# Top-k attention with a highway layer on one core: the joint rest group moved forward, the end of the program re-ordered, a sum moved into SBUF

## The chip, the cores and the metric

The kernel runs on one core of one Trainium2 chip. Its time is the device time of one execution in microseconds (us). Before the change the median of three runs is 880.23 us (879.85 to 880.78). The profiled execution took 880.15 us; its span from the first to the last instruction is 878.4 us, so some 1.8 us lie outside the span.

The engines are named as in the profile: PE is TensorE (PEld its weight loads), DVE is VectorE, ACT is ScalarE, POOL is GpSimd and SP is SyncE, which here only starts transfers.

## What is computed

Inputs are `q`, `k` and `v` of 8 batches, 8 heads, 576 positions and 64 dimensions, and the weights of one layer of width 512. Cut to what matters:

```python
scores = matmul(q, k.T) / sqrt(64)                # (8, 8, 576, 576)
kth    = 32nd largest score of each row
attn   = softmax(where(scores >= kth, scores, -1e9))
x      = matmul(attn, v), heads side by side      # (4608, 512)
H = maximum(x @ w_h, 0)
T = sigmoid(x @ w_t + b_t)
out = T * H + (1 - T) * x                         # (4608, 512) float32
```

The kernel works with `x + (tanh((x @ w_t + b_t) / 2) + 1) * d`, where `d = max(x/2 @ w_h, 0) - x/2`, which is the same value.

## The kernel before

**Tiles and groups.** A batch has 576 queries: four full query tiles of 128 rows and a rest of 64 rows. A `Group` is one query tile of one batch with all its heads. A full group has eight score tiles of 128 queries by 576 keys, one for each head. In a rest group two heads share a tile, 64 rows each, so it has four tiles. The work goes in *pairs* of two tiles: four pairs in a full group, two in a rest group, 144 in all. Two pairs make a *quad*, 72 in all. Two neighbouring batches share the output rows of their rest groups: the second batch's rest group fills rows 64 to 127 of the same buffer, and the *joint* group of 128 rows then goes through the layer once. There are therefore 36 passes through the layer: 32 of full groups and 4 joint ones. The list `groups` (line 762) sets the order, batch by batch, the four full groups and then the rest.

**A pair's way.** PE makes the scores into a PSUM tile of four banks (`scores`, pool `bigps`, one buffer), and ACT moves their positive part into an SBUF buffer `z` (`evac`). Selecting the 32nd largest value of each row is DVE's work. `tree` takes the larger of the two halves of a row (`hi`, one instruction for each pair). `folds` does this twice more for a whole quad (`hh`, `h3`, and the smaller ones into `w2`), and POOL derives the smaller partners in `minima` by exact integer subtraction and addition, four instructions for a quad. `tops` and `rest` are chains of `max` (eight largest values of each row) and `match_replace` over these folded lists. Their last result, `m4`, holds the threshold. `mask` lets ACT write a penalty `pen` for values below it. PE transposes `z` and `pen` together into `zt` and `zr` (`parts`), ACT takes the exponential into `et`, and PE multiplies it with the values (`av`), 20 matmuls of 64 output rows for a pair of a rest group and 10 of 128 for a pair of a full one. ACT copies the result into `xs`.

**The layer of a group.** `norm` takes the reciprocal of the row sums on DVE and multiplies on POOL, which gives `x`. In the loop it then starts the write of `x` to the output in HBM on SP. `ffn_x` transposes `x` on PE, and ACT makes `xT` and `xh`, minus half of `x`. `ffn_h` and `ffn_r` multiply with `w_h` and take the positive part into `d` on ACT, and `ffn_d` adds `xh` to `d` by an accumulating transfer that POOL starts. For joint groups and the last two groups (`late`) one DVE instruction does both. `ffn_t` multiplies with `w_t`, and ACT takes the tanh in PSUM. `ffn_e` (DVE) multiplies, and `ffn_o` adds `d` to the rows already in HBM by accumulating transfers of POOL: one for a full group, two for a joint one, as its rows belong to two batches. The last two groups (`last`) add on an engine instead and write once. For the group before the last, `gp`, DVE also makes the product `x` and `xT`, and POOL makes `xh`.

**What sets the order.** Every engine takes its instructions in program order. The order is written by hand: the loop at line 873 advances one pair in each of 145 steps. In step `n` it folds pair `n`, scores pair `n+1`, selects older pairs, transposes pair `n-4` and multiplies pair `n-5`. `x`, `h` and `t` of the layer are put into a list `ffn` and taken one in each step, `x` in odd steps. If the `t` of one group is followed by the `x` of another, `ffn_x` of the latter is run in the same step, ahead of the transposes of pair `n-4` (lines 895 and 945); this is how a joint group, whose sums are ready two steps after those of the full group ahead of it, comes in. The program behind the loop (lines 960 to 1008) finishes the last three pairs by hand. There `gl` is the last group (before: the joint group of batches 6 and 7, two pairs) and `gp` the one before it (before: the fourth full group of batch 7). Four banks of one `bigps` tile serve as spare PSUM: three for `gp`'s layer, one for the end of the last transposes, and two of them again for `gl`'s `final_t`.

**What decides at the very end** whether the exact second version of the program is needed is computed from `room` and `scales` (`judge_lists`, `judge_scales`, `judge`). It is not needed with these inputs.

Of the kernel before, what the change touches and what calls it, by code (L numbers as in the profile page):

```python
# [9 lines left out]
ALU = mybir.AluOpType  # L10
AX = mybir.AxisListType
FP32 = mybir.dt.float32
# [7 lines left out]
J = 4  # L20
# [47 lines left out]
class Ops:  # L68


    def __init__(self, ctx, tc, shared, exact):
        self.tc = tc
        self.nc = tc.nc if exact else PinnedCore(tc)
        self.__dict__.update(shared)
        self.exact = exact
        s = "g" if exact else ""

        def pool(name, bufs, **kw):
            return ctx.enter_context(tc.tile_pool(name=name + s, bufs=bufs, **kw))

        PS = bass.MemoryType.PSUM
        self.ldpool = pool("ld", 2 if exact else 3)
        self.kqpool = pool("kq", 1 if exact else 2)
        self.scpool = pool("sc", 2) if exact else None
        self.treepool = pool("tree", 3)
        self.wpool = pool("w", 4)
        self.lpool = pool("l", 2)
        self.etpool = pool("et", 2)
        self.xpool = pool("x", 2)
        self.fpool = pool("f", 2)  # L90
        self.bigps = pool("bigps", 1, space=PS)
        self.ztps = pool("ztps", 2, space=PS)
        self.zrps = pool("zrps", 1, space=PS)
        self.fps = pool("fps", 1, space=PS)
        self.st = {}
        self.quads = {}
        self.spare = []

# [147 lines left out]
    def minima(self, k, after):  # L248


        H1, H2 = self.S // 2, self.S // 4
        gp, S = self.nc.gpsimd, self.S
        hi, hh, h3 = self.quads[k]
        z = self.zbufs[k % NZ]
        sci, hii, hhi = [a[:].bitcast(I32) for a in (z, hi, hh)]
        if k == 0:
            head = gp.tensor_tensor(hii, sci[:, :, 0:H1], hii, ALU.subtract)
        else:
            head = gp.tensor_tensor(hhi, hii[:, :, 0:H2], hhi, ALU.subtract)
        self.tc.add_manual_dep(  # L260
            head.ins,
            after.ins.name,
            mybir.DependencyInfo(
                mybir.DependencyClass.Sync, mybir.DependencyReason.DATA
            ),
            reason="after the folds",
        )
        if k:
            gp.tensor_tensor(hhi, hhi, hii[:, :, H2:H1], ALU.add)
            gp.tensor_tensor(hii, sci[:, :, 0:H1], hii, ALU.subtract)  # L270
        gp.tensor_tensor(hii, hii, sci[:, :, H1:S], ALU.add)
# [211 lines left out]
    def norm(self, g):  # L483
        nc, P, H, D = self.nc, self.P, self.H, self.D
        ql = g.rows
        xs3 = g.xs[0:ql, :].rearrange("p (h e) -> p h e", e=D + 1)
        rinv = self.scales[:, g.gi, :]
        nc.vector.reciprocal(rinv[0:ql, :], xs3[:, :, D])
        g.x = self.xpool.tile([P, H * D], FP32, tag="x", name="x")
        x3 = g.x[0:ql, :].rearrange("p (h d) -> p h d", h=H)  # L490
        for hs in (slice(0, H // 2), slice(H // 2, H)) if g.final else (slice(0, H),):
            (nc.vector if g.last else nc.gpsimd).tensor_tensor(
                x3[:, hs, :],
                xs3[:, hs, 0:D],
                rinv[0:ql, hs].unsqueeze(2).to_broadcast([ql, hs.stop - hs.start, D]),
                ALU.mult,
            )
        if g.added:
            for i, dst in enumerate(g.outs):
                n = ql // len(g.outs)  # L500
                nc.sync.dma_start(dst, g.x[i * n : (i + 1) * n, :])

    def final_x(self, g):

# [39 lines left out]
    def final_o(self, g, dsts, queues):  # L544


        vec, P = self.nc.vector, self.P
        W = self.dm // 2
        n = P // len(dsts)
        o = self.fpool.tile([P, self.dm], FP32, tag="o", name="o")  # L550
        for j, tp in enumerate(g.tp):
            cs = slice(j * W, (j + 1) * W)
            vec.scalar_tensor_tensor(
                out=g.d[:, cs], in0=tp, scalar=1.0, in1=g.d[:, cs],
                op0=ALU.add, op1=ALU.mult,
            )
            vec.tensor_tensor(o[:, cs], g.x[:, cs], g.d[:, cs], ALU.add)
            for i, dst in enumerate(dsts):
                queues[i].dma_start(dst[:, cs], o[i * n : (i + 1) * n, cs])

    def ffn_bank(self, g, name, other=False):
        if g.last and not g.final:
            return self.spare.pop(0)
        if g.final or other:
            return self.ztps.tile([self.P, 512], FP32, tag="zt", name=name)
        return self.fps.tile([self.P, 512], FP32, tag="fp", name=name)

    def ffn_x(self, g):
        nc, P, n_g, ql = self.nc, self.P, self.n_g, g.rows
        xtps = self.ffn_bank(g, "xtps", g.joint)  # L570
        for i in range(n_g):
            nc.tensor.transpose(
                xtps[:, i * P : i * P + ql],
                g.x[0:ql, i * P : (i + 1) * P],
                self.ident[0:ql, 0:ql],
            )
        g.xT = self.fpool.tile([P, n_g, P], BF16, tag="xT", name="xT")
        xt3 = xtps[:].rearrange("p (g j) -> p g j", j=P)[:, :, 0:ql]
        if g.last:
            nc.vector.tensor_scalar_mul(g.xT[:, :, 0:ql], xt3, 0.5)  # L580
        else:
            nc.scalar.mul(g.xT[:, :, 0:ql], xt3, 0.5)
        g.xh = self.fpool.tile([P, self.dm], FP32, tag="xh", name="xh")
        if g.last:
            nc.gpsimd.tensor_scalar_mul(g.xh[0:ql, :], g.x[0:ql, :], -0.5)
        else:
            nc.scalar.mul(g.xh[0:ql, :], g.x[0:ql, :], -0.5)

    def ffn_h(self, g):
        nc, P, n_g, ql = self.nc, self.P, self.n_g, g.rows  # L590
# [63 lines left out]
    def ffn_o(self, g, *dsts):  # L654
        ql = g.rows
        n = ql // len(dsts)
        if g.added:
            for i, dst in enumerate(dsts):
                self.nc.gpsimd.dma_start(
                    dst, g.d[i * n : (i + 1) * n, :], accum_op=ALU.add  # L660
                )
            return
        o = self.fpool.tile([self.P, self.dm], FP32, tag="o", name="o")
        self.nc.gpsimd.tensor_tensor(o[0:ql, :], g.x[0:ql, :], g.d[0:ql, :], ALU.add)
        for i, dst in enumerate(dsts):
            self.nc.sync.dma_start(dst, o[i * n : (i + 1) * n, :])
# [3 lines left out]
def kernel(  # L670
# [10 lines left out]
    nc = tc.nc  # L681
    P = nc.NUM_PARTITIONS
    B, H, S, D = q.shape
# [8 lines left out]
    nck = J + 1  # L692
# [21 lines left out]
    for i in range(2):  # L714
# [15 lines left out]
        P=P, H=H, S=S, D=D, R=R, NHP=NHP, n_g=n_g, dm=dm,  # L730
# [5 lines left out]
    with ExitStack() as cm:  # L736
# [18 lines left out]
        def out_rows(g):  # L755
            if not g.rem:
                r0 = g.b * S + g.qt
                return [out[r0 : r0 + JP : J, :]]
            ends = [(g.b + i) * S for i in (0, 1)]
            return [out[r1 - R : r1, :] for r1 in ends]  # L760
# [1 line left out]
        groups = [  # L762
            Group(b, qt, b * nck + qt, H, P, joint=True)
            for b in range(B)
            for qt in range(nck)
        ]
        groups[-1].final = True
        for i, g in enumerate(groups):
# [95 lines left out]
        def attend(m):  # L864
            ops.mask(m, *pairs[m])
            values(m - 1)
            ops.trans(m)

        def values(m):
            g, pi = pairs[m]  # L870
            ops.av(m, g, pi, preps[g.b]["vb"])

        while step <= NPR:
# [83 lines left out]
                ffn += [("x", g), ("h", g), ("t", g)]  # L957
            step += 1

        (kind, fg), = ffn  # L960
        assert kind == "t" and not pieces
        m, (gp, gl) = NPR - 3, groups[-2:]
        ops.ffn_t(fg)
        attend(m)
        late = ops.lists_rest(m // 2 + 1, *pairs[m + 1])
        gens, late = late[0:2], late[2:]
        ops.run(gens)
        ops.mask(m + 1, *pairs[m + 1])
        ops.ffn_e(fg)
        ops.ffn_o(fg, *out_rows(fg))  # L970
        ops.run(late)
        big = ops.bigps.tile([P, 2, 1024], FP32, tag="big", name="ps")
        banks = [
            big[:, i // 2, i % 2 * 512 : (i % 2 + 1) * 512] for i in range(4)
        ]
        ops.spare = banks[0:3]
        values(m)
        part, ends = ops.parts(m + 1)
        part(0)
        ops.mask(m + 2, *pairs[m + 2], tis=(0,))  # L980
        part(1)
        ops.mask(m + 2, *pairs[m + 2], tis=(1,))
        ends()
        ops.norm(gp)
        ops.settle(gl)
        part, ends = ops.parts(m + 2, banks[3])
        ends()
        part(0)
        values(m + 1)
        ops.ffn_x(gp)  # L990
        part(1)
        judge_lists()
        values(m + 2)
        ops.norm(gl)
        ops.ffn_h(gp)
        ops.ffn_r(gp)
        ops.final_x(gl)
        ops.ffn_d(gp)
        ops.ffn_t(gp)
        judge_scales()  # L1000
        ops.ffn_e(gp)
        ops.ffn_o(gp, *out_rows(gp))
        ops.ffn_h(gl)
        ops.ffn_r(gl)
        ops.ffn_d(gl)
# [78 lines left out]
```

## Time and profile before

| view of the profile | what it shows |
|---|---|
| busy share of the span | DVE 96%, PE 80%, ACT 79%, POOL 79% |
| windows of 110 us between 112 and 772 us | DVE busy 109.31 to 109.38 us in each |
| window 834 to 846 us | DVE busy 11.73 of 12.00 us |
| window 846 to 860 us | DVE busy 10.18 of 14.00 us |
| window 860 us to the end | DVE busy 8.39, PE 7.56, ACT 3.56 us |
| last selecting instruction of DVE (`m`) | ends at 856.39 us |
| last compute instruction (`o` on DVE) | ends at 872.19 us |
| granted PE clock | 0.954 over the span, 0.80 from 860 us on |

All compute instructions pass through one helper, so they carry line 35, and the profile's groups are told apart by the names of their tiles: `hh<-hi` is a fold, `x<-xs,scales` the product of `norm`, `d<-hps,xh` the `ffn_d` of a joint group. A group's row reads: engine, operation, output and input with shapes, how often; then busy time in us, mean ns of one; then the time the engine was idle ahead of them and who ended that. A timeline's row reads: start in us, duration in us, engine and instruction, and in brackets the idle time ahead of it and its releaser. Durations of instructions that follow each other on an engine overlap a little, as they are pipelined; from start to start a `d` costs DVE 0.59 us though its duration is 0.69.

### The profile page before, as it was taken

The page shows a single profiled execution, that of the slowest core. Times are in us where ns is not written, and L with a number is a line of the kernel's source. Part 1 is how long each engine was busy: PE and PEld are TensorE (multiplying, and loading weights), DVE is VectorE, ACT ScalarE, POOL GpSimd, SP SyncE. Part 2 cuts the span into 40 slices and gives each one's busy share as a digit, 9 for nine tenths or more (in the row PEclk, how much of TensorE's full clock was granted, in tenths as well). Part 3 has the DMA queues.
Part 4 walks back from the last instruction along what each step waited for, and adds up shares of the span by engine and source line. Part 5 has one row for each costly group of instructions (what it writes and reads, how often), then busy time and mean ns, then how long its engine had stood idle before and what let it go on. Part 6 is the DMA issues. An engine that isn't in the chain of part 4 may idle for free.

```text
span 878.4 us, 19848 instructions
## 1 busy us (share of the span) xinstructions
PE 704.7 (80%) x6524; PEld 497.8 (57%) x6569; DVE 847.3 (96%) x4201; ACT 694.9 (79%) x1243; POOL 695.8 (79%) x451
## 2 busy tenths in 40 slices
PE   6777988878787888778788787887988778877884
PEld 4555565655555556555566555665655555655652
DVE  4999999999999999999999999999999999999994
ACT  4787978888788897788788887887878888777873
POOL 5788887888878888788887888888887888878861
PEclk9799999999999999999999999999999999898888
DMA  9553413233143332234234341223313211111121
GB/s 201 123 109 69 102 37 61 67 65 89 29 85 69 72 84 49 62 59 102 41 70 76 67 108 24 52 66 73 97 38 61 38 34 29 38 25 25 38 40 37
DMA packets 104702, 57.32 MB, mean 65 GB/s; under 512 B 82192, under 2 KB 91792, under 8 KB 104592
## 3 DMA queue, kind: packets, MB, share of 16 engines
q1 hardware_dynamic: 92768, 37.37, 16.7%
q0 software_dynamic: 10608, 18.22, 13.7%
q8 instruction: 53, 0.87, 0.4%
q10 hardware_dynamic: 1216, 0.39, 0.2%
q14 instruction: 57, 0.47, 0.2%
HBM read 30.67 MB, written 18.35 MB: 56 GB/s over the span
## 4 chain that ended last, share of the span: by engine, by line
DVE 93%; PE 2%; ACT 2%; issue 1%; SPq 1%; DMA 0%; DVEq 0%; ACTq 0%
DVE w L35 50%; DVE m L35 19%; DVE hi L35 11%; DVE hh L35 7%; DVE h L35 4%; DVE d L35 3%; PE ps L35 1%; PE zt L35 1%; ACT pen L35 1%; SPq L35 1%; ACT et L35 0%; DMA qin<-in_q_dram 0%; DVE scales L35 0%; ACT z L35 0%; PE zr L35 0%
## 5 line engine op out<-in xcount | busy, mean ns | idle before, releaser
L35 PE MATMUL ps<-kq 64*128 64x64 f32 (+3 forms) x1280 | 215.9, 463 | 93.5 <-DVE hi L35 89.2
L35 ACT ACTIVATE z<-ps 128x1152 f32<-128x1152 f32 x144 | 163.2, 1134 | 111.3 <-PE ps L35 108.9
L35 ACT ACTIVATE pen<-z,m 128x576 bf16<-128x576 f32 x288 | 226.2, 786 | 0.1
L35 PE MATMUL zt<-ident,z 128*128 128x128 f32 x1152 | 223.4, 287 | 0.3
L35 PEld LDWEIGHTS ps<-kq 64*128 64x128 f32 (+1 forms) x1280 | 108.7, 186 | 194.4 <-DVE hi L35 100.4
L35 PE MATMUL zt<-nident,pen 128*128 128x128 bf16 x1152 | 212.8, 224 | 0.0
L35 POOL TENSOR_TENSOR hh<-hi,hh 128x576 int32<-128x576 int32 x71 | 100.4, 1414 | 133.4 <-DVE w L35 133.4
L35 POOL TENSOR_TENSOR hi<-z,hi 128x1152 int32<-128x1152 int32 x72 | 189.4, 2631 | 14.0 <-DVE m L35 8.5
L35 POOL TENSOR_TENSOR hi<-hi,z 128x1152 int32<-128x1152 int32 x72 | 191.1, 2654 | 5.6
L35 PEld LDWEIGHTS zt<-ident,z 128*128 128x128 f32 x1152 | 168.4, 146 | 18.3 <-ACT xT L35 1.0
L35 ACT ACTIVATE et<-zt 128x512 bf16<-128x512 f32 x288 | 161.4, 606 | 12.3 <-PE zt L35 11.5
L35 DVE MAX8 m<-w 128x8 f32<-128x168 f32 x576 | 161.1, 323 | 0.0
L35 PEld LDWEIGHTS <-pen 128*128 128x128 bf16 x1440 | 159.1, 111 | 2.9 <-ACT pen L35 2.8
L35 DVE MAX8 w<-hi 128x8 f32<-128x288 f32 x288 | 116.8, 448 | 0.1
L35 DVE TENSOR_TENSOR hi<-ps,z 128x576 f32<-128x576 f32 x144 | 108.0, 750 | 5.8 <-ACT z L35 5.8
L35 POOL TENSOR_TENSOR hh<-hh,hi 128x576 int32<-128x576 int32 x71 | 100.2, 1411 | 5.6
L35 PE MATMUL zr<-v,et 128*128 128x65 bf16 (+1 forms) x1580 | 89.4, 196 | 18.6 <-ACT et L35 14.7
L35 PEld LDWEIGHTS <-et 128*128 128x128 bf16 (+1 forms) x1600 | 70.0, 102 | 59.5 <-ACT et L35 45.4
L35 DVE MATCH_REPLACE8 w<-m,w 128x168 f32<-128x168 f32 x288 | 89.7, 321 | 0.0
L35 DVE MAX8 w<-hh 128x8 f32<-128x72 f32 x576 | 85.2, 234 | 0.0
L35 PE MATMUL zr<-ident,z 128*128 128x128 f32 x286 | 73.9, 312 | 2.3 <-ACT xs L35 2.3
L35 DVE TENSOR_TENSOR hh<-hi 128x576 f32<-128x576 f32 x73 | 58.6, 803 | 2.5
(91 smaller groups left out, 1120.9 us busy)
## 6 DMA issues: line engine op xcount, KB each, us to landing
vin<-in_v_dram SPq DMA_DIRECT2D x8, 1024.0 KB, 5.6
kin<-in_k_dram SPq DMA_DIRECT2D x63, 128.0 KB, 3.1
qin<-in_q_dram SPq DMA_DIRECT2D x63, 128.0 KB, 3.1
out_dram<-x SPq DMA_DIRECT2D x31, 256.0 KB, 2.9
d<-xh POOLq DMA_DIRECT2D x31, 256.0 KB, 3.6
out_dram<-d POOLq DMA_DIRECT2D x31, 256.0 KB, 4.2
krest<-in_k_dram SPq DMA_DIRECT2D x8, 128.0 KB, 3.9
qrest<-in_q_dram SPq DMA_DIRECT2D x8, 128.0 KB, 4.9
```

Of the source, the lines that this page charges most:

```text
L35: return self._tc.keep_in_program_order(fn(*args, **kw))
```

## The change

1. In the last batch the rest group is taken second, after the first full group. The joint group of batches 6 and 7 then passes through the layer in the loop, like the other three, and the last two groups `gp` and `gl` are both full.
2. Behind the loop `bigps` is closed and four one-bank PSUM tiles take its place. `gp`'s layer starts right behind the loop and is spread over the last three pairs; `gl`'s layer follows alone. ACT makes `xT` and `xh` of `gp`, and POOL its `x`.
3. The product `x` of a joint group is not started in `norm`. It is kept (`due`) until the next quad's `minima`, where it stands ahead of them, and behind that quad's folds.
4. A joint group's `x` is no longer written to HBM and added to there. POOL starts one transfer that adds `d` to `x` in SBUF, and SP then writes the sum in two transfers.
5. In `final_o` each half of the columns has a queue of its own (one transfer for a full group's 128 rows), where before each destination had.

Its aim is to end with a group whose tiles are shorter to score and multiply, to take `gp`'s layer out of the last stretch, and to keep POOL's product from DVE's folds.

```diff
@@ pools
-        self.bigps = pool("bigps", 1, space=PS)
+        self.bigctx = ctx.enter_context(ExitStack())
+        self.bigps = self.bigctx.enter_context(
+            tc.tile_pool(name="bigps" + s, bufs=1, space=PS)
+        )
+        self.due = None
@@ minima
+        due, self.due = self.due, None
+        lead = self.norm_x(due) if due else None
...
+        head = lead or head          # the first one waits for the folds
@@ norm
+        if g.joint and g.added and not self.exact:
+            self.due = g
+        else:
+            self.norm_x(g)
+
+    def norm_x(self, g):
...
-            (nc.vector if g.last else nc.gpsimd).tensor_tensor(
+            made = (nc.vector if g.final else nc.gpsimd).tensor_tensor(
...
-        if g.added:
+        if g.added and not g.joint:
             (write x to the output on SP)
@@ final_o
-                queues[i].dma_start(dst[:, cs], o[i * n : (i + 1) * n, cs])
+                queues[j].dma_start(dst[:, cs], o[i * n : (i + 1) * n, cs])
@@ ffn_x
-        if g.last:
-            nc.vector.tensor_scalar_mul(g.xT[:, :, 0:ql], xt3, 0.5)
-        else:
-            nc.scalar.mul(g.xT[:, :, 0:ql], xt3, 0.5)
+        nc.scalar.mul(g.xT[:, :, 0:ql], xt3, 0.5)
...
-        if g.last:
-            nc.gpsimd.tensor_scalar_mul(g.xh[0:ql, :], g.x[0:ql, :], -0.5)
-        else:
-            nc.scalar.mul(g.xh[0:ql, :], g.x[0:ql, :], -0.5)
+        nc.scalar.mul(g.xh[0:ql, :], g.x[0:ql, :], -0.5)
@@ ffn_o
+        if g.added and g.joint:
+            self.nc.gpsimd.dma_start(g.x[0:ql, :], g.d[0:ql, :], accum_op=ALU.add)
+            for i, dst in enumerate(dsts):
+                self.nc.sync.dma_start(dst, g.x[i * n : (i + 1) * n, :])
+            return
@@ groups
-            for qt in range(nck)
+            for qt in (range(nck) if b < B - 1 else [0, J, *range(1, J)])
@@ behind the loop
-        ops.ffn_t(fg)
+        ops.bigctx.close()
+        (tail pool: banks = four tiles of one bank)
+        ops.spare = banks[0:3] + [None]
         attend(m)
+        ops.ffn_x(gp)
         (first half of the last lists); ops.mask(m + 1, *pairs[m + 1])
-        ops.ffn_e(fg)
-        ops.ffn_o(fg, *out_rows(fg))
+        ops.ffn_h(gp)
         ops.run(late)
-        (banks = four views of one bigps tile)
+        ops.settle(gl)
         values(m)
+        ops.ffn_r(gp)
+        ops.ffn_d(gp, ops.ffn_t(gp))
         (transposes of pair m + 1, masks of pair m + 2)
-        ops.norm(gp)
-        ops.settle(gl)
         part, ends = ops.parts(m + 2, banks[3])
+        part(0)
         ends()
-        part(0)
+        ops.ffn_e(gp)
+        ops.ffn_o(gp, *out_rows(gp))
         values(m + 1)
-        ops.ffn_x(gp)
         part(1)
         judge_lists()
         values(m + 2)
         ops.norm(gl)
-        ops.ffn_h(gp)
-        ops.ffn_r(gp)
         ops.final_x(gl)
-        ops.ffn_d(gp)
-        ops.ffn_t(gp)
         judge_scales()
-        ops.ffn_e(gp)
-        ops.ffn_o(gp, *out_rows(gp))
+        ops.spare = [ops.fps.tile([P, 512], FP32, tag="fp", name="hps")]
         ops.ffn_h(gl)
         ops.ffn_r(gl)
         ops.ffn_d(gl)
```

## The prediction

> **What bounds the kernel now.** I read the chain of waits first, then the groups, then timelines. The chain, by engine, with the row of the folds:
>
> ```profile
> DVE 93%; PE 2%; ACT 2%; issue 1%; SPq 1%; DMA 0%; DVEq 0%; ACTq 0%
> ...
> L35 DVE TENSOR_TENSOR hh<-hi 128x576 f32<-128x576 f32 x73 | 58.6, 803 | 2.5
> ```
>
> DVE alone sets the time up to the end of selection: among its timeline rows I find only one wait between 22 and 850 us, 0.20 us. In the loop only DVE time counts. The mean fold is 803 ns although its median is 759; so I listed all 73 folds. Sixty-seven take 0.76 or 0.77 us, six take 1.17, 1.41, 1.21, 1.43, 1.19 and 1.39. The timeline around the first two, POOL and DVE, and an ordinary one:
>
> ```profile
> 229.15 1.31 POOL L35 TENSOR_TENSOR x<-xs,scales 128x512 f32<-128x512 f32 x1
> 230.49 0.77 DVE L35 TENSOR_TENSOR hh<-hi 128x576 f32<-128x576 f32 x1
> ...
> 241.09 1.32 POOL L35 TENSOR_TENSOR x<-xs,scales 128x512 f32<-128x512 f32 x1
> 241.86 1.17 DVE L35 TENSOR_TENSOR hh<-hi 128x576 f32<-128x576 f32 x1
> ...
> 264.74 1.69 POOL L35 DMA_DIRECT2D out_dram<-d  x2
> 265.91 1.59 POOL L35 TENSOR_TENSOR x<-xs,scales 128x512 f32<-128x512 f32 x1
> 266.71 1.41 DVE L35 TENSOR_TENSOR hh<-hi 128x576 f32<-128x576 f32 x1
> ```
>
> An ordinary product ends 0.03 us before the fold. Twice for each joint group it doesn't: its own product starts late (241.09), and that of the next full group stands behind the joint group's two transfer starts (264.74) and starts 1.17 us after them. Both pairs overlap, and the fold pays.
>
> The end, by DVE's timeline, then PE's and ACT's:
>
> ```profile
> 853.44 0.69 DVE L35 SCALAR_TENSOR_TENSOR d<-tps,d 128x512 f32<-128x512 f32 x1 [0.90 <-DMA d<-xh]
> 860.66 0.69 DVE L35 TENSOR_SCALAR xT<-ps 128x512 bf16<-128x512 f32 x1 [3.40 <-PE ps L35]
> 867.40 0.69 DVE L35 SCALAR_TENSOR_TENSOR d<-ps,d 128x512 f32<-128x512 f32 x1 [1.22 <-ACT ps L35]
> 870.51 0.42 DVE L35 SCALAR_TENSOR_TENSOR d<-ps,d 128x256 f32<-128x256 f32 x1 [1.46 <-ACT ps L35]
> ...
> 868.14 0.60 PE L35 MATMUL ps<-wt,xT 128*128 128x256 bf16 x4 [0.47 <-DVE d L35]
> 869.31 0.60 PE L35 MATMUL ps<-wt,xT 128*128 128x256 bf16 x4 [0.46 <-ACT ps L35]
> ```
>
> Here DVE waits: for a transfer in the middle of the last selection, then for PE and ACT. PE's two rows are `final_t`'s halves. The first waits for `gp`'s `d` and the second for the first half's tanh, neither of which it needs; all use views of one PSUM tile.
>
> **What the Trainium skill says.** "SBUF — State Buffer", section Who interferes with whom: a DVE instruction with two SBUF inputs contends with a GpSimd instruction that reads SBUF, and one with a single SBUF input does not. The trace agrees for folds (0.55 us of overlap cost 0.41, 0.79 cost 0.65), and `max` runs beside POOL's minima unharmed. "DMA: Bandwidth & Descriptors", section Anatomy of one DMA, gives 2.0 us and bytes over 436e3 for a transfer started by GpSimd: an estimate of 2.6 us for 256 KB. The trace has a median of 3.6 for `d<-xh`, which I use. "PSUM — Partial Sum Buffer", section Terms: two engines must not touch one bank at once. `final_t`'s halves lie in two banks, so the waits above come from the tile, not from this rule; no run here shows a collision.
>
> **The loop, part by part.**
> - Folds: 0.41 + 0.65 + 0.45 + 0.67 + 0.43 + 0.63 = 3.24 us of excess over 0.76. Deferring the joint product puts it behind the folds, where DVE runs `max`, and reads of PSUM with one SBUF input. One transfer start instead of two brings the next product forward by 0.6 us (starts follow by 0.61: 240.48 to 241.09), to about 265.3, ending at 266.65, 0.06 ahead of the fold. I count -3.24; lower end -1.3, the first, third and fifth only.
> - The fourth joint group is now `late` in the loop: one more `d<-hps,xh` on DVE ahead of the selection's end, +0.59. `ffn_e`s up to that end are equal in number: 34.
> - The wait of 0.20 for `z` at 839.30 goes: it follows 16 score matmuls of a rest group that took 3.82 us; a full group's eight take 1.3.
> - The deferred product delays that quad's four minima by 1.4 us. POOL waits 1.6 to 3.0 us for folds around there (1.56 at 243.97, 3.04 at 256.45), so it catches up: 0. Behind it PE holds `ffn_x` of the joint group, now released at about 244.95 instead of 243.33, and behind that the transposes of pair n-4, ACT's exponentials, the next scores. These end in `z`, started at 250.81, which DVE needs at 253.97: of 3.16 us, 1.14 is its length and 1.6 the delay. It fits with 0.4 to spare, since PE also has two waits of 0.8 and 0.67 there. I count 0, upper end 1.6 for each of four groups.
> - The sum in SBUF: one 3.6 us transfer, then writes of 3.0. SP's loads stand behind its wait, but are used three steps (17 us) later: 0. `x` stays occupied longer; its second buffer is next wanted two groups on: 0.
>
> **The end of selection.** It comes at 856.39. Off go 3.24, 0.20 and the 0.90 (the `ffn_e` in question moves into the loop, its transfer long landed); on come 0.59, and 0.11 for `gp`'s reciprocal, formerly behind it: 852.75, a gain of 3.64.
>
> **From there to the last `o`.** Before, 15.8 us. After, two chains meet, and I add up instruction by instruction. POOL ends the last minima at 850.14 - 2.85 = 847.3; one transfer start 0.6 and `gp`'s product 1.32 give 849.3. PE's transposes, 0.65, ACT's `xT`, 0.55, `ffn_h`, 1.0, `av` of ten matmuls, 0.5, and `ffn_t`, 1.25, give 853.3. Then ACT is the engine in turn: tanh, two 512-wide exponentials, two `pen`s (m4 is ready at 852.75), a third exponential, two short ones and one `xs` copy: 0.5 + 3 x 0.49 + 2 x 0.67 + 2 x 0.27 + 0.2 = 4.05, 857.4. Behind stand PE's second transposes of the last tile, 0.7, its exponential, 0.6, ten `av` matmuls, 0.5, the copy, 0.3, and the reciprocal, 0.2: `gl`'s product starts at 859.7 to 859.8, where before it started at 863.37. DVE's `d` and `ffn_e` of `gp`, 1.3, run beside ACT: 0.
>
> From that product before, 8.82 us passed to the end at 872.19. After: `xT` 1.73 as before (863.37 to 865.10), 861.5; `ffn_h` 1.0, 862.5; first half of `final_t` 0.72 and the second, with banks of its own, 0.72 at once behind, with `judge`'s transpose 0.2 ahead, 864.1; its tanh 0.4, 864.5. DVE's `d` ends at 863.2 and the flag at 863.6. The first half of `final_o` starts at 863.9, four instructions of 0.43 give 865.6. `gp`'s `ffn_t` (1.25), the `ffn_e` that held DVE, and the two false waits have gone. Last writes: two of 128 KB instead of four of 64; 256 KB took 2.3 and 64 KB 2.5 to 2.7 us, so 0.
>
> **Sum.** 872.19 - 865.6 = 6.6, of which 3.64 before the end of selection and 3.0 behind: 880.23 - 6.6 = 873.6.
>
> **Rivals.**
> - *The next group's product still meets the fold.* Its clearance is 0.06 us by my own working. Then 0.65 + 0.67 + 0.63 = 1.95 come back: 875.6. For: the thin margin, and a transfer into SBUF may take POOL longer to start. Against: ordinary products, with one start ahead, clear all 28 times.
> - *The tail gives nothing.* `gp`'s layer puts tanh, `xT` and `xh`, 1.6 us of ACT, ahead of the last masks, and PE waits in order for POOL's product. PE's clock could fall in these waits: 16 score matmuls took 3.81 us at 834 and 2.17 at 828. If this eats all 3.0: 880.23 - 3.64 = 876.6. Against: `gp`'s matmuls and false waits are gone from behind `gl`'s product, and the last thresholds are there at 852.75, some 1.8 us before ACT reaches their masks.
> - *Slower: the deferral stalls DVE.* If PE's 1.6 us reaches `z` at all four joint groups, +6.4, and ACT's 1.0 to 1.6 us of extra work at the end delays rather than gains, +1.0: 880.23 - 3.64 + 6.4 + 1.0 = 884.0. For: PE and ACT show no wait over 0.8 us in this stretch. Against: the spare 0.4, and DVE needs `z` alone.
> - *Half of that* cancels the gain: about 880.3.
>
> **Chances.** Forecast 0.55; fold still met 0.14; loop only 0.20; cancelled 0.04; slower 0.07. The last two are what I leave out, with little at the edges. The lower end takes 1.5 us more from a PE at full clock in the tail and shorter waits: 872.0. The upper reaches past 876.6: 877.2. Faster 0.89, same 0.04, slower 0.07.
>
> **What would show it.** All folds at 0.76 us, and no DVE wait on `z` in the loop. POOL's product behind the folds four times. Last `m` near 852.8, `gl`'s product near 859.8, last `o` near 865.6; `final_t`'s second half starting without a wait for ACT. I am wrong if three folds stay at 1.4, if DVE waits for `z` or PE near 243, or if PE runs at half clock from 850 on.

## The result, and the profile after

The changed kernel takes 874.51 us (median of four, 872.87 to 875.65) against 880.11 us for the kernel before (its three runs of the first section and one more), 5.6 us less: a ratio of 0.9934, 95% interval [0.9917, 0.9951]. The profiled execution has a span of 872.9 us against 878.4.

The page's first line and the chain's shares by engine:

```profile
span 872.9 us, 19884 instructions
...
DVE 90%; PE 4%; POOL 2%; DMA 1%; issue 1%; ACT 1%; SPq 0%; DVEq 0%; POOLq 0%; ACTq 0%
```

From the trace's answer on the tile `hh`, the folds (durations in ns: least, median, most; then the first and last start in us):

```profile
L35 DVE TENSOR_TENSOR hh<-hi x73: 757/758/760, 15.3 to 839.4; 128x576 f32<-128x576 f32 x73
```

No fold is long any more: the longest of 73 takes 760 ns, where six took up to 1428. DVE still carries the chain, with more of PE and POOL in it. The timelines of POOL and DVE around the first joint group show why:

```profile
243.16 0.76 DVE L35 TENSOR_TENSOR hh<-hi 128x576 f32<-128x576 f32 x1
244.33 0.45 DVE L35 TENSOR_TENSOR w<-hh 128x288 f32<-128x288 f32 x1
244.94 1.03 POOL L35 TENSOR_TENSOR x<-xs,scales 128x512 f32<-128x512 f32 x1 [2.31 <-PE zr L35]
...
265.63 0.85 POOL L35 DMA_DIRECT2D x<-d  x1
266.25 1.32 POOL L35 TENSOR_TENSOR x<-xs,scales 128x512 f32<-128x512 f32 x1
267.60 0.76 DVE L35 TENSOR_TENSOR hh<-hi 128x576 f32<-128x576 f32 x1
```

The joint product now starts behind the last fold. The next group's product has one transfer start ahead of it instead of two and ends at 267.57, 0.03 us before its fold.

The end, from DVE's timeline:

```profile
861.21 0.20 DVE L35 RECIPROCAL scales<-xs 128x8 f32<-128x8 f32 x1 [2.82 <-ACT xs L35]
861.58 0.76 DVE L35 TENSOR_TENSOR x<-xs,scales 128x256 f32<-128x256 f32 x2 [0.17 <-DVE scales L35]
864.65 0.69 DVE L35 SCALAR_TENSOR_TENSOR d<-hps,xh 128x512 f32<-128x512 f32 x1 [0.85 <-PE hps L35]
866.33 0.42 DVE L35 SCALAR_TENSOR_TENSOR d<-t,d 128x256 f32<-128x256 f32 x1 [0.63 <-ACT t L35]
867.80 0.43 DVE L35 TENSOR_TENSOR o<-x,d 128x256 f32<-128x256 f32 x1
```

`gl`'s sums come 2.82 us after DVE asks for them; then its longer waits are for PE's product `hps` and for the first tanh, for which ACT waits for PE. PE's timeline:

```profile
864.56 1.06 PE L35 MATMUL t<-wt,xT 128*128 128x256 bf16 x4
865.62 1.06 PE L35 MATMUL t<-wt,xT 128*128 128x256 bf16 x4
```

The two halves of `final_t` follow each other without a wait, but each group of four matmuls takes 1.06 us, where it took 0.60 before. Granted PE clock is 0.63 between 864 and 868 us.

The following stretches are read from the timelines of each profile; every number is a difference of two rows. "Loop" runs from the start of `tree` of pair 3 to that of pair 118, ahead of all that the new order moves. "End" runs from the start of `tree` of the last pair, 143, to the end of the last `o`; "product to o" is its last part, from the start of `gl`'s product. "Writes" is the rest of the span, which is known to 0.1 us.

| kernel | loop | end | product to o | writes | time, us |
|---|---|---|---|---|---|
| before | 672.34 | 32.89 | 8.82 | 6.21 | 880.11 |
| changed | 669.28 | 29.59 | 6.65 | 4.67 | 874.51 |
| loop_only | 669.26 | 32.76 | 8.81 | 5.80 | 877.65 |
| end_only | 672.26 | 30.93 | 6.84 | 4.79 | 877.03 |
| hbm_sum | 671.43 | 33.37 | 6.53 | 4.75 | 877.15 |
| at_once | 670.47 | 29.32 | 5.36 | 5.41 | 877.12 |
| one_tile | 669.44 | 31.55 | 8.07 | 4.97 | 875.53 |
| four_writes | 669.20 | 29.33 | 5.37 | 5.78 | 875.26 |
| keep_warm | 670.06 | 28.34 | 5.37 | 5.43 | 873.38 |
| keep_warm_b | 669.14 | 29.63 | 5.36 | 5.40 | 872.82 |
| dve_x_warm | 669.19 | 28.75 | 5.36 | 4.66 | 873.41 |
| x_first_warm | 669.65 | 27.62 | 5.37 | 5.58 | 872.85 |

Two stretches lie outside the table: the start up to pair 3 (21.73 us before, 23.05 in the changed kernel) and the way from pair 118 to pair 143 (145.24 and 146.31). With them the sum closes: 3.06 + 3.30 + 1.54 - 1.32 - 1.07 = 5.51 us, the difference of the two spans.

The time is a median over several runs, the stretches are those of one of them. That matters: runs of the changed kernel differ by up to 2.8 us, so the times alone separate little below 1 us, and the verdicts below rest on rows.

### The profile page after: what moved, and what is told of

Same layout as the page of the kernel before. It is cut to its first block, busy times and chain, and to the rows that moved or that the text cites. A ratio compares the mean times of both kernels' runs of the same rounds, so it can differ in the third digit from the quotient of the medians.

```text
span 872.9 us, 19884 instructions
## 1 busy us (share of the span) xinstructions
PE 707.8 (81%) x6569; PEld 500.4 (57%) x6569; DVE 843.6 (97%) x4200; ACT 695.9 (80%) x1244; POOL 690.8 (79%) x447
## 4 chain that ended last, share of the span: by engine, by line
DVE 90%; PE 4%; POOL 2%; DMA 1%; issue 1%; ACT 1%; SPq 0%; DVEq 0%; POOLq 0%; ACTq 0%
DVE w L35 48%; DVE m L35 18%; DVE hi L35 11%; DVE hh L35 6%; DVE h L35 4%; DVE d L35 3%; PE ps L35 1%; POOL hi L35 1%; PE zt L35 1%; POOL hh L35 1%; PE t L35 1%; DMA d<-xh 1%; DMA qrest<-in_q_dram 1%; PE zr L35 1%; ACT z L35 1%
## 5 line engine op out<-in xcount | busy, mean ns | idle before, releaser
L35 PE MATMUL ps<-kq 64*128 64x64 f32 (+3 forms) x1280 | 212.1, 457 | 89.5 <-DVE hi L35 85.4
L35 PE MATMUL zt<-ident,z 128*128 128x128 f32 x1152 | 225.7, 289 | 0.1
L35 PE MATMUL zt<-nident,pen 128*128 128x128 bf16 x1152 | 215.0, 225 | 0.3 <-ACT pen L35 0.3
L35 PE MATMUL zr<-nident,pen 128*128 128x128 bf16 x286 | 59.8, 230 | 0.3 <-ACT pen L35 0.3
```

The costliest lines, as they stand in the source:

```text
L35: return self._tc.keep_in_program_order(fn(*args, **kw))
```

## Experiments

**The loop's edits alone.** The kernel before, with products of joint groups deferred and their sums in SBUF:

```diff
@@ the kernel before
+        (minima: due, norm and norm_x, ffn_o for joint groups as in the change)
```

> The kernel before with the change's two loop edits alone: joint products behind the folds, joint sums in SBUF, for the first three joint groups; order of the last batch and end as before. Theory (the six long folds are the loop's whole gain): all folds at 0.76 us, 3.2 us less than before, about 876.9 us. Rival (the deferral costs as much elsewhere, so that the change's gain comes from its end): within 1 us of before.

Measured: 877.65 us, ratio to before 0.9965 [0.9952, 0.9977], 3.0 us less by the medians of this comparison (880.6 before). No fold is long:

```profile
L35 DVE TENSOR_TENSOR hh<-hi x73: 757/758/762, 15.2 to 837.4; 128x576 f32<-128x576 f32 x73
```

The loop is 3.08 us shorter than before and the end within 0.13. This is the theory's case: a little over half of the change's gain comes from six folds.

**The rest of the change alone.** The changed kernel without those two edits:

```diff
@@ the changed kernel
-        if g.joint and g.added and not self.exact:
+        if False:                                   # product at once
...
-        if g.added and not g.joint:
+        if g.added:                                 # x of joint groups written, too
...
-        if g.added and g.joint:
-            (sum into x in SBUF, two writes)
```

> The changed kernel without the two loop edits: joint products at once, joint sums by adding in HBM. Theory: eight long folds, two for each of the four joint groups, 4 x 1.06 = 4.2 us slower than the changed kernel, about 878.7 us, and the end as in the changed kernel. Rival (gain from the end only): as the changed kernel, 874.5 us.

Measured: 877.03 us, ratio 0.9951 [0.9933, 0.9968]. Eight folds take 1.17 to 1.42 us, two for each of four joint groups, and the loop is as long as before (672.26). The time lies between the theory's 878.7 and the rival's 874.5. The rows show the four groups' eight long folds, so the loop part is settled. The 3.6 us less than this comparison's 880.6 come from the end and the last writes, with the fourth joint group's two long folds counted against them.

**Each loop edit undone by itself.** First the sums in HBM again, products still deferred:

```diff
@@ the changed kernel
-        if g.added and not g.joint:
+        if g.added:                                 # x of joint groups written, too
...
-        if g.added and g.joint:
-            (sum into x in SBUF, two writes)
```

> The changed kernel with joint sums in HBM again, so that POOL starts two transfers for each; products still deferred. Theory (the second start pushes the next full group's product into the fold): four folds of 1.4 us, 4 x 0.65 = 2.6 us slower than the changed kernel, about 877.1 us. Rival (the start time has nothing to do with the fold): no change.

Measured: 877.15 us, ratio 0.9951 [0.9932, 0.997]. Exactly four folds are long, 1.42, 1.38, 1.39 and 1.36 us, all in the quad of the next full group's product, as expected. The loop, which holds three of them, is 2.15 us longer than in the changed kernel: 1.91 us of it is fold, and `ffn_e` has a wait of 0.35 us at 457 us, which is looked at below. The end of this profile is 3.8 us longer than in the changed kernel, which the edit doesn't explain: its granted clock was 0.50 from 848 to 856 us.

Then products at once, sums in SBUF:

```diff
@@ the changed kernel
-        if g.joint and g.added and not self.exact:
+        if False:
```

> The changed kernel with joint products at once in norm, sums in SBUF. Theory: four folds of about 1.19 us, 4 x 0.43 = 1.7 us slower than the changed kernel, about 876.2 us. Rival (the deferral holds PE at the joint groups and costs DVE time, among it the 0.36 us wait for z at 768 us): faster than the theory by what DVE no longer waits, 0.4 us or more, or even faster than the changed kernel.

Measured: 877.12 us, ratio 0.9956 [0.9942, 0.9971]. Again exactly four folds are long, the other ones, 1.17, 1.18, 1.20 and 1.18 us; the loop is 1.19 us longer for three of them. So each long fold belongs to one edit. The medians alone would not have told this: with one edit undone, with the other and with both (877.15, 877.12 and 877.03 us) they are the same, though four, four and eight folds are long. The rival finds nothing in the rows: the wait for `z` at 768 us is absent here, but it is absent in five profiles of kernels with the new order that defer as well, and no deferred product stands near it (those of the changed kernel are at 244.94, 454.78, 664.66 and 805.16). Another wait, of 0.35 to 0.71 us, stands ahead of an `ffn_e` at 457 us in three of the nine profiles of kernels that defer (hbm_sum, keep_warm, x_first_warm), and in none of the three that don't. It is not the deferral's: in all three `ffn_e` starts 0.08 to 0.12 us after the landing of a transfer `d<-xh`, which took 5.5 to 5.9 us there (3.6 and 3.8 in the median of the two main profiles), and which starts at the same point with and without deferral, 5.0 us behind `tree` of pair 76.

**PSUM by tile or by bank.** The changed kernel with its four banks as views of one tile:

```diff
@@ the changed kernel
-        banks = [tail.tile([P, 512], ...) for i in range(4)]
+        big = tail.tile([P, 2, 1024], FP32, tag="t", name="t")
+        banks = [big[:, i // 2, i % 2 * 512 : (i % 2 + 1) * 512] for i in range(4)]
```

> The changed kernel with the end's four PSUM banks as views of one tile again. Theory (waits by tile, not by bank): final_t's second half waits for the first's tanh (0.46 us before) and final_o's first half for the second tanh; at the end 0.5 to 1.5 us slower than the changed kernel, and more waits in the transposes of the last pair. Rival (the banks' separation is hidden by other work): same time, no wait of that kind.

Measured: 875.53 us, ratio 0.9942 [0.9927, 0.9957]. PE's and DVE's timelines have the old waits again:

```profile
863.07 1.49 PE L35 MATMUL hps<-wh,xT 128*128 128x512 bf16 x3 [0.58 <-DVE ok L35]
864.56 1.06 PE L35 MATMUL t<-wt,xT 128*128 128x256 bf16 x4
866.35 0.60 PE L35 MATMUL t<-wt,xT 128*128 128x256 bf16 x4 [0.52 <-ACT t L35]
...
867.56 0.42 DVE L35 SCALAR_TENSOR_TENSOR d<-t,d 128x256 f32<-128x256 f32 x1 [1.85 <-ACT t L35]
```

PE waits 0.52 us for the first half's tanh ahead of `final_t`'s second half, and DVE waits for the second tanh ahead of `final_o`'s first half. From product to last `o` it is 8.07 us, 1.42 more than in the changed kernel, both with a lowered clock. The rival falls by the rows; the times, 1.0 us apart, agree but don't separate the two.

**The last writes.** The changed kernel with four writes of 64 rows, two on each queue:

```diff
@@ final_o
-            for i, dst in enumerate(dsts):
-                queues[j].dma_start(dst[:, cs], o[i * n : (i + 1) * n, cs])
+            for i in range(2):
+                r = slice(i * P // 2, (i + 1) * P // 2)
+                queues[i].dma_start(dsts[0][r, cs], o[r, cs])
```

> The changed kernel with its last rows written in four transfers of 64 rows, two on each queue, as before, instead of two of 128 rows. Theory (the second start on a queue and its later landing make the 6.2 us between the last o and the end, 4.7 in the changed kernel): 1 to 1.5 us between the last o and the end come back. Rival (that time varies by itself): 4.7 us as in the changed kernel.

Measured: 875.26 us, ratio 0.9945 [0.993, 0.996]. After the last `o` pass 5.78 us. The last `o` and the last start on each queue, and below them the same of the changed kernel:

```profile
865.80 0.42 DVE L35 TENSOR_TENSOR o<-x,d 128x256 f32<-128x256 f32 x1
866.25 0.47 SPq L580 DMA_DIRECT2D out_dram<-o  x1
866.25 1.27 ACTq L35 DMA_DIRECT2D out_dram<-o  x1
...
867.80 0.43 DVE L35 TENSOR_TENSOR o<-x,d 128x256 f32<-128x256 f32 x1
868.25 0.36 ACTq L35 DMA_DIRECT2D out_dram<-o  x1
```

The second start on a queue does not come late: with four writes and with two, the last start begins 0.03 us behind the last `o` (in the kernel before at 872.22, behind 872.19). It takes longer, 0.47 and 1.27 us here and 0.50 and 0.65 in the kernel before, against 0.36. But neither expectation holds alone: the nine profiles with two writes have 4.66 to 5.58 us behind the last `o` (median 4.97), the three with four writes 5.78, 5.80 and 6.21. So about 0.8 us go with the number of writes, by three profiles against nine; how is not shown, as the last write lands 3.16 to 3.24 us behind the last `o` with four writes and 2.00 to 3.32 with two. The rest of the 1.5 us between the two main profiles varies by itself.

**The clock at the end.** The changed kernel with transposes of the identity into an unused bank, put where PE waits:

```diff
@@ behind the loop, and in its last step
+        def keep(n):
+            for _ in range(n):
+                ops.nc.tensor.transpose(fill[:, 0:P], ident[:], ident[:])
...
+        keep(8)              # ahead of the transposes of pair 140
+            keep(5)          # and of pair 141
+        keep(4)
         ops.ffn_x(gp)
+        keep(3)
         ops.ffn_h(gp)
+        keep(3)
         values(m + 2)
+        keep(7)
         ops.norm(gl)
```

> The changed kernel with 30 transposes of the identity into a free PSUM bank, put where PE waits from 842 us on (8, 5, 4, 3, 3 and 7), none of them used. Theory (the end varies and misses the forecast because the granted clock falls to half while PE waits in it): granted clock 1.0 from 842 us to the last matmul, last selection to last o in 12.9 us or less (13.7 in the changed kernel's profile), and about 1 us less time, 873.5 us, with less spread. Rival (the clock falls for another reason, or the fillers hold the real matmuls up): clock as before and time the same or up to 1 us slower.

Measured: 873.38 us (873.01 to 874.12), ratio 0.9919 [0.9905, 0.9933]. The same stretch of PE's timeline, and the windows of the two kernels (length in us, busy us of PE, PEld, DVE, ACT and POOL, granted clock, share of the DMA engines, GB/s), first of keep_warm:

```profile
863.98 0.60 PE L35 MATMUL t<-wt,xT 128*128 128x256 bf16 x4
864.53 0.60 PE L35 MATMUL t<-wt,xT 128*128 128x256 bf16 x4
...
856.00:864.00 8.00, 6.66 (x69) 4.85 (x69) 4.42 (x12) 5.21 (x12) 1.28 (x1) 1.00 0.10 35
864.00:868.00 4.00, 1.24 (x12) 0.86 (x9) 2.63 (x7) 0.74 (x2) 0.00 (x0) 1.00 0.16 53
```

and of the changed kernel:

```profile
856.00:864.00 8.00, 5.58 (x58) 3.83 (x57) 4.48 (x12) 5.29 (x12) 1.27 (x1) 0.97 0.09 33
864.00:868.00 4.00, 2.90 (x13) 1.57 (x11) 2.50 (x7) 0.74 (x2) 0.00 (x0) 0.63 0.01 4
```

With a clock of 1.0 the last 6.65 us become 5.37, which is also what every other profile with this end and the full clock there has. A second measurement of the same kernel:

> keep_warm once more, on the same chip as x_first_warm. Expected: 873.4 us, granted clock 1.0 to the last matmul, 12.4 us from last selection to last o.

It gave 872.82 us, ratio 0.9906 [0.9891, 0.9921], and again 5.36 us. But the granted clock was 0.79 between 840 and 848 us, and the end took 29.63 us, as long as without fillers (13.74 of them from the last selection to the last `o`). PE's timeline shows that the eight fillers of that stretch came late: their bank was still being read by `ffn_e`.

```profile
842.67 1.82 PE L35 MATMUL fill<-ident 128*128 128x128 f32 x8 [1.54 <-DVE d L35]
```

So the wait that they were to fill stayed. But in keep_warm they come just as late, at 843.84 behind a wait of 1.53 us, and the clock stays at 1.0. The difference is where the wait falls. In all twelve traces the granted clock is either 1.0 or 0.5 (a mean between them is a mixture) and changes only on a grid of steps of 3.41 us, which lies differently in each execution. Two steps of keep_warm_b, then of keep_warm:

```profile
839.45:842.87 3.42, 1.52 (x20) 1.02 (x19) 3.42 (x13) 2.24 (x5) 2.88 (x3) 1.00 0.05 8
842.87:846.28 3.41, 3.41 (x21) 3.04 (x21) 3.41 (x24) 0.95 (x2) 3.33 (x2) 0.50 0.01 2
...
839.35:842.77 3.42, 2.42 (x29) 1.72 (x27) 3.38 (x12) 1.84 (x4) 1.69 (x2) 1.00 0.45 77
842.77:846.18 3.41, 2.34 (x25) 2.25 (x26) 3.41 (x15) 2.18 (x5) 3.33 (x2) 1.00 0.01 2
```

In keep_warm_b the whole wait lies in one step, which leaves PE busy for 1.52 of 3.41 us, and the next step has half the clock; in keep_warm a step ends within the wait, and PE is busy for 2.42 and 2.34 us. Counted over the twelve traces, none of the 2203 steps at full clock with PE busy for 68% or more was followed by one at half clock, and 146 of the 148 below 50% were; in between both occur. This is a count and not an experiment. A lowered clock is thus shown to lengthen the end; the fillers do not reliably prevent it, and their gain in time, 1.1 to 1.7 us by medians, is not beyond the intervals.

**Who holds the end's chain.** `gp`'s product on DVE, fillers as before except the four ahead of `ffn_x(gp)`:

```diff
@@ norm_x
-            made = (nc.vector if g.final else nc.gpsimd).tensor_tensor(
+            made = (nc.vector if g.last else nc.gpsimd).tensor_tensor(
```

> As keep_warm without its four transposes at 851 us, and with gp's product on DVE, as in the kernel before. Theory (the end's chain runs through POOL's minima and its product, on which PE waits 0.90 us): gp's x ready near 848.3 instead of 851.3, PE's transposes 1 us earlier, DVE's selection 0.6 us later but off that chain: 0.5 to 1.0 us less than keep_warm. Rival (DVE's selection sets the end): 0.6 us more than keep_warm.

Measured: 873.41 us, ratio 0.9922 [0.9909, 0.9936]: neither better nor worse. DVE's timeline with the product, and POOL's beside it:

```profile
847.21 2.35 DVE L35 TENSOR_TENSOR x<-xs,scales 128x512 f32<-128x512 f32 x1
...
846.36 2.65 POOL L35 TENSOR_TENSOR hi<-hi,z 128x1152 int32<-128x1152 int32 x1
```

The product took 2.35 us, where DVE did it in 0.73 in the kernel before, beside one POOL instruction of 0.22 us. It ended 0.55 us after POOL's instruction: it had waited for it, as the folds had. The Trainium skill ("SBUF — State Buffer", section Who interferes with whom) has the port pair that DVE and GpSimd share locked by one of them at a time, and lets the order of issue decide who blocks; this row agrees, as POOL had started first and the product lost 1.62 of the 1.80 us for which it ran beside it. `gp`'s `x` was ready at 849.56, not 848.3, and selection ended 2.1 us later than in keep_warm; the two cancelled. Both theories misjudged the cost of the move.

The other way to the same end is POOL's order:

```diff
@@ the loop's last two steps
                 if kind == "t":
                     ops.ffn_e(fg)
-                    ops.ffn_o(fg, *out_rows(fg))
+                    (in the last but one step: kept as held)
...
                     ops.norm(pairs[n - 5][0])
+                if n == NPR:
+                    ops.ffn_o(held, *out_rows(held))
```

> As keep_warm without its four transposes at 851 us; POOL starts the transfer of the group before gp behind gp's product instead of ahead of it. Theory (the end's chain runs through POOL's last minima, this transfer start and the product): product 0.6 us earlier, PE's transposes of gp's x 0.6 us earlier, last selection to last o 0.4 to 0.6 us shorter than keep_warm's 12.4, time 0.3 to 0.6 us less. Rival (ACT or DVE holds the end by then): product earlier, end no earlier than 0.1 us.

Measured: 872.85 us, ratio 0.9905 [0.9889, 0.9921]. POOL's timeline:

```profile
848.67 1.04 POOL L35 TENSOR_TENSOR x<-xs,scales 128x512 f32<-128x512 f32 x1
849.65 0.85 POOL L35 DMA_DIRECT2D out_dram<-d  x1
```

The product follows the last minima at once; last selection to last `o` is 11.71 us against keep_warm's 12.44, and the whole end is 0.72 us shorter. The chain did run through the transfer start: PE's transposes of `x` come 0.70 us earlier against `tree` of the last pair, with the full clock in both ends. (The four fillers that keep_warm has ahead of them end 0.10 us before its product and delay nothing.) The time equals that of keep_warm_b beside it (872.82): a gain of this size is seen in the rows and not in the medians. Both lie below the changed kernel's 874.51, with intervals that overlap its own.

## Why the prediction was right, and what it missed

Forecast 873.6 us, range 872.0 to 877.2; measured 874.51. By its steps:

- **Folds, -3.24.** Right. The loop lost 3.06 us; loop_only, hbm_sum and at_once show each long fold with its cause. The feared meeting of the next product and the fold did not come: it clears it by 0.03 us, where the working had 0.06.
- **The deferral, 0.** Right but for one wait. PE does wait for the deferred product (1.55 us at the fourth joint group of the changed profile), but only there did it reach DVE, with 0.22 us at 812.36, where the clock was 0.5 from 805.51 to 812.34.
- **The rest group's scores, -0.20.** Mis-sized. The working removed the wait at 839 us and gave the group's new place none. There DVE waited 0.36 us for `z` (767.99), as in two other profiles, 0.37 and 0.53. It goes with the clock: the last stretch at half clock ahead of it ended 7.8 to 10.6 us before that `tree` in these three (from 750.89 to 757.72 us here), and 11.2 us or more before it in the seven others of this order. No run separates the two, so the cause is argued, not shown. One more `d`, +0.59, is as forecast: from pair 131 to pair 143 six profiles without other waits have 0.27 to 0.31 us more than before, against 0.39 forecast.
- **End of selection at 852.75.** It was at 854.53, 1.78 late. Of this 1.32 is the start of the run: `tree` of pair 3 starts at 23.05 us here and at 21.73 in the profile before, and anywhere from 21.89 to 22.98 in the ten others, all of the same code up to there. That part is not the change's. The rest is 0.18 in the loop and 0.68 between pairs 118 and 143 more than worked out, less 0.41 that the last pair's selection took less.
- **From there to `gl`'s product, 7.0.** Measured 7.05. The chain is the one worked out: last minima, transfer start, POOL's product, PE, and then ACT and PE in turn. PE waited 0.90 us for it.
- **From the product to the last `o`, 5.8.** Measured 6.65, and 5.36 or 5.37 in the six profiles whose last products ran at the full clock. The step took full-clock durations for PE, and was 0.4 us too long for these; the clock's fall, which was named only for a rival, cost 1.3 us. The profile before had the full clock there: the 0.80 of the first part's table averages in the half clock from 872.13 us on, behind the last matmul, and from 860 us up to there it was 1.0. So the lower end of the range, in so far as it hoped for a faster PE there, had nothing to win. The false waits went as forecast; one_tile brings them back.
- **Last writes, 0.** Wrong in the change's favour: 1.54 us between the two profiles, of which about 0.8 goes with the number of writes. The working took the landing times of single transfers for all that differs; by what way the number acts is not shown.

So the mechanism was right, and that the size came so close is in part luck: in the two profiles the steps before the writes came out 2.7 us worse than worked out, half of it in the start of the run, and the writes 1.5 us better. The two sources, half loop and half end, are what loop_only and end_only show. How the end's 3.3 us divide between the moved rest group and the re-ordered layer of `gp` no run separates; of its edits only the banks' own tiles (one_tile) and the writes were tried alone.

## What to carry to other kernels

A group's mean that lies above its median is worth a list of its members: here six of 73 folds showed two scheduling faults whose repair gave more than half of the gain. Before two engines' operands are moved about, look at what the other engine runs in that window; a product that cost 0.73 us with POOL all but idle cost 2.35 beside its minima. At the end of a program, work the chain out by instruction, separate PSUM banks into tiles of their own, and allow for a PE clock that falls when PE has waited for much of one step of 3.41 us, which one execution meets and the next does not.

## What had not been expected of the hardware

- A DVE product with two SBUF inputs, started 0.85 us into a POOL instruction of 2.65 us, ended 0.55 us after it (2.35 us in all). For the folds this was known; that it blocks a whole product for most of POOL's instruction was not.
- Granted PE clock at the end differs from one execution of the same program to the next, and short waits suffice to lower it. In hbm_sum it was 1.0 up to 846 us and 0.50 from 847 to beyond 856, though PE's longest wait since 840 us had been 1.63 us, for ACT's copy `xs`. The Trainium skill ("TensorE: Matmul & The Clock Gate", section Part 1: The HAM clock gate) tells of a half and a full rate, set by PE's recent activity in a free-running window of about 3.4 us, and of a fall after an idle window. The two rates and the free-running steps of 3.41 us agree with these traces. An idle window in the sense of one without work does not: in the step ahead of the fall PE was busy for 1.31 us (hbm_sum), 1.52 (keep_warm_b) and 1.54 (changed).
- Time to `tree` of pair 3 varies by 1.3 us with the same code (21.73 to 23.05 us). The first `tree` already varies by 0.75 us (9.81 to 10.56). The rest goes with the same steps of the clock: where its first fall to half comes at 21.0 us or later (four profiles), DVE waits 0.21 us ahead of pair 3; where it comes earlier the wait is longer, up to 1.21 us with a fall at 19.3.
